# A fused attention-and-MLP decode step with its gradients: one product moved in the forward loop, two stores moved in the backward loop

## The chip, the core and the metric

The kernel runs on one NeuronCore of a Trainium2 chip. Its five engines work side by side, each through its own queue of instructions in order: PE (matrix products), DVE and ACT (vector and scalar work), POOL and SP (here they issue DMAs). Sixteen DMA engines move data between HBM and SBUF. The metric is the device time of one execution in microseconds; lower is better.

## The reference

One token `x` of width D = 640 passes through a layer with adaptive layer norm: attention over a cache, then an MLP. The attention has 32 heads of width 192, and each head has its own K and V cache of 8192 rows. The reference computes the output and the gradients of nine inputs.

```python
def _A_ref(x, k_cache, v_cache, wq, wo):          # 1 query, 32 heads, 8192 rows, 192 wide
    q = (x @ wq).reshape(B, Sq, Hq, Dh) ...
    scores = einsum('bhqd,bhkd->bhqk', q, k) * Dh ** (-0.5)
    p = softmax(scores)
    o = einsum('bhqk,bhkd->bhqd', p, v)
    return o.reshape(B, Sq, Hq * Dh) @ wo
mod = silu(c) @ w_mod                             # sa, ca, ga, sb, cb, gb
h = layernorm(x) * (1 + ca) + sa
x = x + ga * _A_ref(h, K, V, wq, wo)
h = layernorm(x) * (1 + cb) + sb
x = x + gb * _B_ref(h, w1, w2, w3, w4)            # with one token: h + gelu(layernorm(h) @ w3) @ w4
# returned: x, and the gradients of A_x, K, V, wq, wo, w3, w4, c, w_mod for a given grad_out
```

K and V are 2 x 32 x 3.1 MB and must be read; their gradients have the same size and must be written. V is read a second time for the backward part. The gradients of `wq`, `wo` and `w_mod` are outer products of two vectors and are written once each.

## The kernel before

**Layout.** A head's 8192 rows lie on 128 partitions with 64 rows each. A head is loaded in two halves of 32 rows (1.5 MB each); K goes through five such buffers (`KB`), V through three (`VB`).

**Forward loop** (lines 505 to 591, `i` from 0 to 30). The order of the instructions on PE, DVE, ACT and SP is the order of the source lines (`manual_schedule`). An iteration works on three heads at once: the scores of head `i` (`x`), the weighted sums of head `i - 1` (`y`), and the end of head `i - 2` (`z`). The scores of a half are a product on DVE (`dot_mul`, L303), a halving add on DVE (`dot_half`, L308), a sum by matmuls with the identity on PE (`dot_tree`, L314) and a last sum on DVE (`dot_sum`, L318). Softmax takes the maximum through a PE transpose (`mx`, L520) that DVE reads (`negm`, L526), and exponentials on ACT (L349). The weighted V (`scale_v`) is made a quarter at a time, 9 of 16 rows on DVE (L362) and 7 on ACT (L369). For each quarter PE then runs `m_quarter`: the matrix M = K' diag(p) V, which the backward part uses (L384, L389), and the output o (L401). The fourth quarter of a head runs in the next iteration.

In odd iterations from 3 on, the two heads of a pair `t` are finished: `pair_sum` (L438 to 440, PE) sums their outputs into `po`, `pair_o` (L444 to 448, four small DVE operations) divides by the softmax sums, and `pair_ao` (L455, 15 small matmuls) multiplies by the pair's rows of `wo`. The copy of the product (L558, ACT) and the copies of the next query (L273) or modulation (L245) are put into the list `late` and run after the fourth `scale_v`; the products they copy (`q_mm`, L268, in iterations with `i % 4` of 3 and 0; `mod_mm`, L241, at 2, 6 and 10) run where the list is filled. `q_ps` and `mx` share one PSUM buffer (pool `psB`, tag "b", one buffer). SP issues the loads in source order: the next `wo` block (L211) waits until `pair_ao` has read an old one, and the V load of line 582 stands behind it.

**Backward loop** (lines 1231 to 1279, 64 half heads `s`). Each half head needs dP = dO V' (DVE L931, PE L940, DVE L318), then dS (L1239), dK as an outer product on DVE (L956), and dV as outer products on PE (L951) that ACT copies out (L952). Both are stored by DMAs that POOL issues (`store`, L1189), dV of a half head first, and then dK. Beside them runs a list of side jobs, which `slot()` advances in even steps over the half heads: among them `g_chunk`, which turns a loaded block of `wq` or `w_mod` into the block of its gradient in place (in the buffers `w_st` and `stg` in turn) and stores it (L1050). The last two of these blocks are columns 0 and 1 of `w_mod`. POOL also loads rows of probabilities for later half heads (`er_b`, L795).

Of the kernel before, what the change touches and what calls it, by code (L numbers as in the profile page):

```python
# [20 lines left out]
def kernel(  # L21
# [26 lines left out]
    nc = tc.nc  # L48
# [16 lines left out]
    CW = 2 * PW  # L65
# [48 lines left out]
    def tcol(n, name, dtype=FP32):  # L114
        return tmp.tile([P, n], dtype, name=name)
# [81 lines left out]
    dwm_v = out_9.rearrange("(i p) n -> p i n", p=P)  # L197
# [5 lines left out]
    def load_w(view3, lo, hi):  # L203
        w = wst.tile([P, ND, CW], BF16, name="w_st", tag="w", bufs=1)
        nc.sync.dma_start(out=w[:, :, 0 : hi - lo], in_=view3[:, :, lo:hi])
        return w
# [99 lines left out]
    def dot_half(prod):  # L306
        w = DH // 2
        V_.tensor_tensor(out=prod[:, :, 0:w], in0=prod[:, :, 0:w], in1=prod[:, :, w : 2 * w], op=ALU.add)  # L308

    def dot_tree(prod, psR, w):  # L310

        ps = psR.tile([P, JH, TS], FP32, name="dot_ps", tag="d")
        for k in range(0, w, TS):
            T_.matmul(ps, lhsT=ident_bf, rhs=prod[:, :, k : k + TS], start=(k == 0), stop=(k == w - TS))  # L314
        return ps

    def dot_sum(ps, dst):
        V_.reduce_sum(out=dst, in_=ps, axis=AX.X)  # L318
# [20 lines left out]
    with tc.tile_pool(name="vs", bufs=3) as vsp, tc.tile_pool(name="ft", bufs=2) as ft, \  # L339
# [7 lines left out]
        def softmax(h, S_h, negm):  # L347
            E4 = ft.tile([P, J, 4], BF16, name="E4")
            A_.activation(out=E4, in_=S_h[:, :, None].to_broadcast([P, J, 4]), func=ACT.Exp, bias=negm[:, 0:1], scale=1.0)  # L349
            A_.copy(out=E_all[:, h, :], in_=E4[:, :, 0])  # L350
            Ef = ft.tile([P, J], FP32, name="Ef")
            A_.copy(out=Ef, in_=E4[:, :, 0])
            return E4, Ef

        def g_scale_v(q, v, E4, Ef, out, n):
            vs = vsp.tile([P, JQ, VW], BF16, name="vs")
            out.append(vs)
            j0 = q * JQ
            v0 = (q % 2) * JQ
            A_.copy(out=vs[:, :, DH:VW], in_=E4[:, j0 : j0 + JQ, :])  # L360
            if n:
                V_.tensor_tensor(  # L362
                    out=vs[:, 0:n, 0:DH].rearrange("p j (a b) -> p j a b", b=4),
                    in0=v[:, v0 : v0 + n, :].rearrange("p j (a b) -> p j a b", b=4),
                    in1=E4[:, j0 : j0 + n, None, :].to_broadcast([P, n, DH // 4, 4]),
                    op=ALU.mult,
                )
            for k in range(n, JQ):
                A_.activation(out=vs[:, k, 0:DH], in_=v[:, v0 + k, :], func=ACT.Copy, scale=Ef[:, j0 + k : j0 + k + 1])  # L369
                yield  # L370

        def scale_v(q, v, E4, Ef, n=JQ - NVA):
            out = []
            for _ in g_scale_v(q, v, E4, Ef, out, n):
                pass
            return out[0]

        def m_units(q, kb, vs, mp, last=3):
            j0 = (q % 2) * JQ
            z = q == last  # L380

            def main(lo, hi):
                for k in range(lo, hi):
                    T_.matmul(mp[:, 0:MW], lhsT=kb[:, j0 + k, 0:P], rhs=vs[:, k, 0:MW], start=(q == 0 and k == 0), stop=(z and k == JQ - 1), skip_group_check=True)  # L384

            def rest():
                for k in range(JQ):
                    p0 = 64 * (k % 2)
                    T_.matmul(mp[p0 : p0 + 64, MO : MO + MW], lhsT=kb[:, j0 + k, P:DH], rhs=vs[:, k, 0:MW], start=False, stop=(z and k >= JQ - 2), skip_group_check=True)  # L389

            return [lambda: main(0, JQ // 2), lambda: main(JQ // 2, JQ), rest]

        def m_quarter(q, kb, vs, mp, op):
            for f in m_units(q, kb, vs, mp):
                f()
            o_quarter(q, vs, op)

        def o_quarter(q, vs, op):
            for k in range(JQ):
                p0 = 32 * (k % 4)  # L400
                T_.matmul(op[p0 : p0 + 32, 0:MW], lhsT=ones_bf, rhs=vs[:, k, 0:MW], start=(q == 0 and k < 4), stop=(q == 3 and k >= JQ - 4), skip_group_check=True)  # L401
# [40 lines left out]
        def pair_o(t, po):  # L442
            rz = tcol(3, "rz")
            V_.reciprocal(out=rz, in_=po[:, 3:6])  # L444
            V_.tensor_scalar(out=o_col[:, 3 * t : 3 * t + 3], in0=po[:, 0:3], scalar1=rz[:, 0:1], scalar2=None, op0=ALU.mult)
            V_.tensor_copy(out=rinv[:, 2 * t : 2 * t + 2], in_=rz[:, 1:3])
            o2 = ft.tile([P, 3, 2], BF16, name="o2")
            V_.tensor_tensor(out=o2, in0=omask, in1=o_col[:, 3 * t : 3 * t + 3, None].to_broadcast([P, 3, 2]), op=ALU.mult)
            return o2
# [8 lines left out]
        w = load_w(wq_v, 0, CW)  # L458
# [44 lines left out]
        with tc.manual_schedule(engines=ORDER):  # L503
            for i in range(H1):
                x = X.get(i)
                nx = X[i + 1] = {"k": [], "v": []}
                y = X.get(i - 1) if i > 0 else None
# [16 lines left out]
                if y is not None:  # L524
                    negm = tcol(1, "negm")
                    V_.reduce_max(out=negm, in_=mx, axis=AX.X, negate=True)  # L526
                    E4, Ef = softmax(i - 1, y["S"], negm)
# [21 lines left out]
                    m_add(i - 2, z["mp"], mt)  # L549
                dot_half(pb)  # L550
                x["d1"] = dot_tree(pb, psR, DH // 2)
                if last:
                    o2 = pair_o(t, po)
                if y is not None:
                    vs = scale_v(2, y["v"][1], E4, Ef)
                if last:
                    ps_ao = pair_ao(o2, wo_l.pop(t))
                    late.append(lambda ps=ps_ao, t=t: A_.copy(out=AO[:, :, 2 * t : 2 * t + 2], in_=ps))  # L558
# [13 lines left out]
                if i % 4 == 0 and mb < NMB:  # L572
                    nb = min(CW // P, NMB - mb)
                    wch = load_w(wm_v, mb * P, (mb + nb) * P)
                if y is not None:
                    m_quarter(2, y["k"][1], vs, y["mp"], y["op"])
                dot_sum(x["d0"], x["S"][:, 0:JH])
                if y is not None:
                    y["vs"] = scale_v(3, y["v"][1], E4, Ef)
# [16 lines left out]
            x, y, z = X[H1], X[H1 - 1], X[H1 - 2]  # L596
# [191 lines left out]
    NS = 2 * HQ  # L788
# [22 lines left out]
    def transposed(x0, cols, outer, wT):  # L811

        n = min(8, 15 - x0)
        tp = psT.tile([P, 1024], BF16, name="wT_ps", tag="t")
        for x in range(x0, x0 + n):
            b, a = divmod(x, outer)
            for lo, hi, src in cols(a, b):
                T_.transpose(out=tp[lo:hi, (x - x0) * P : (x - x0 + 1) * P], in_=src, identity=ident_bf)  # L818
        A_.copy(out=wT[:, x0 * P : (x0 + n) * P], in_=tp[:, 0 : n * P])  # L819
# [146 lines left out]
    HEADS = ((0, 0, P, 0), (1, 0, 64, P), (2, 0, P, DH), (1, 64, P, DH + P))  # L966
    NWM = NMOD // CW
    GX = -(-2 * ND // 6)
    cur = {}
    wseq = []  # L970

    def next_w():
# [40 lines left out]
    def g_chunk(b, first, v3, rows, dst, n, acc, lay):  # L1013

        lo = n * CW
        if first:
            cur["w"] = cur.pop("next")
        w = stg = cur["w"][:, :, b * PW : (b + 1) * PW]
        cols = lambda a, b_: [(l, r, w[:, a, c0 : c0 + r - l]) for bb, l, r, c0 in lay if bb == b_]
        v_bf = tcol(3, "v_bf", BF16)  # L1020
        V_.tensor_copy(out=v_bf, in_=v3)
        yield
        wT = bst.tile([P, 15 * P], BF16, name="wT", tag="wT")
        transposed(0, cols, ND, wT)
        tp = psS.tile([NF, P], FP32, name="bc_t", tag="s")
        T_.transpose(out=tp[0:3, :], in_=v3, identity=ident_f)
        vrow = tmp.tile([3, P], BF16, name="vrow")
        A_.copy(out=vrow, in_=tp[0:3, :])
        yield
        transposed(8, cols, ND, wT)  # L1030
        bp = psB.tile([P, 512], FP32, name="bc_ps", tag="b")
        for bb, l, r, c0 in lay:
            T_.matmul(bp[:, c0 : c0 + r - l], lhsT=pick(3, bb), rhs=vrow[:, l:r], start=True, stop=True)
        v_bc = bst.tile([P, PW], BF16, name="v_bc")
        A_.copy(out=v_bc, in_=bp[:, 0:PW])
        yield
        ps = psS.tile([P, ND], FP32, name="acc_ps", tag="s")
        for i in range(ND):
            for bb in range(3):
                T_.matmul(ps[:, i : i + 1], lhsT=wT[:, (bb * ND + i) * P : (bb * ND + i + 1) * P], rhs=v_bf[:, bb : bb + 1], start=(bb == 0), stop=(bb == 2))  # L1040
        for i in range(3):
            V_.tensor_scalar(out=stg[:, i, :], in0=v_bc, scalar1=rows[:, i : i + 1], scalar2=None, op0=ALU.mult)
        yield
        V_.tensor_tensor(out=acc, in0=ps, in1=acc, op=ALU.add)
        for i in range(3, ND):
            V_.tensor_scalar(out=stg[:, i, :], in0=v_bc, scalar1=rows[:, i : i + 1], scalar2=None, op0=ALU.mult)
        if first:
            next_w()
        else:
            nc.gpsimd.dma_start(out=dst[:, :, lo : lo + CW], in_=cur["w"])  # L1050
        yield

    def g_dq(t):
# [96 lines left out]
    NP = sum(n for n, _ in jobs)  # L1150
    side = iter(p for _, g in jobs for p in g)
    SLOTS = 4 * (NS - 5)
    prog = [0, 0]
# [77 lines left out]
    for s in range(NS):  # L1231
# [8 lines left out]
            out=dS4,  # L1240
# [36 lines left out]
            dq_cols(s, row)  # L1277
        done_s[0] = s + 1
        slot()
    while prog[1] < NP:  # L1280
        next(side)
        prog[1] += 1


# [28 lines left out]
```

## Time and profile before

| | |
|---|---|
| median of 7 runs | 1438.03 us (1435.35 to 1441.87) |
| profiled execution, its time | 1439.51 us |
| profiled execution, its span | 1437.7 us |
| busy: PE, DVE, ACT, POOL | 1194.2, 1110.4, 878.8, 138.0 us |
| moved by DMA | 571.96 MB, mean 398 GB/s |
| mean granted PE clock | 0.714 |

The span reaches from the first to the last instruction of the trace. Busy times are sums of instruction times, and for PE the ends are modelled. "Idle before" is the time in which an engine stood still ahead of an instruction, with what released it. The chain of work that ended last has PE 36%, DVE 29%, DMA 13%, issue 9% and ACT 9% of the span.

### The profile page before, as it was taken

The numbers are of one execution on the slowest core, as the hardware profiler recorded it, in microseconds if no ns is written. First come the engines' busy times: TensorE is split into PE (matmuls) and PEld (weight loads), VectorE is DVE, ScalarE is ACT, GpSimd is POOL, SyncE is SP. The second block draws the span as 40 slices with busy tenths as digits, with TensorE's granted clock in tenths as the row PEclk, the third lists the DMA queues.
The fourth block names the chain that finished last, engine by engine and source line by source line (L and its number), as shares of the span: only waits on it lengthen the run. The fifth ranks groups of instructions, "written<-read, shape, count | busy, mean of one in ns | idle before, by whom it ended". The sixth has DMA issues, their size and how long they took to land.

```text
span 1437.7 us, 29992 instructions
## 1 busy us (share of the span) xinstructions
PE 1194.2 (83%) x12577; PEld 779.9 (54%) x12577; DVE 1110.4 (77%) x1395; ACT 878.8 (61%) x1923; POOL 138.0 (10%) x240
## 2 busy tenths in 40 slices
PE   3999999999999897888888787877787788778984
PEld 1677777777777676544444444444444444444542
DVE  4999999999999996676766776676677567667683
ACT  0777777677777763545565656556566556555654
POOL 0000000000000000111110111111111111111111
PEclk7999999999999997655555556556556555555555
DMA  9999999999999995699999999999999999999997
GB/s 374 402 419 419 417 417 413 412 407 416 417 410 410 418 382 198 242 399 422 415 403 422 420 413 415 418 419 421 391 417 423 400 414 397 412 383 409 393 412 324
DMA packets 77748, 571.96 MB, mean 398 GB/s; under 512 B 8590, under 2 KB 26718, under 8 KB 37294
## 3 DMA queue, kind: packets, MB, share of 16 engines
q1 hardware_dynamic: 51402, 343.59, 59.0%
q0 software_dynamic: 26192, 226.47, 38.2%
q8 instruction: 98, 1.61, 0.4%
q14 instruction: 36, 0.29, 0.0%
q10 hardware_dynamic: 20, 0.00, 0.0%
HBM read 343.58 MB, written 225.91 MB: 396 GB/s over the span
## 4 chain that ended last, share of the span: by engine, by line
PE 36%; DVE 29%; DMA 13%; issue 9%; ACT 9%; POOL 1%; SPq 0%; ACTq 0%; POOLq 0%; DVEq 0%
PE dot_ps L940 16%; DVE prod L303 9%; DMA out_dram<-KB 7%; PE dv_ps L951 6%; DVE pq L931 5%; DMA KB<-in_A_k_cache_dram 4%; DVE vs L362 4%; PE wT_ps L818 4%; DVE prod L308 4%; ACT vs L369 3%; PE mp L384 3%; PE dot_ps L314 2%; DVE S_h L318 2%; ACT wT L819 2%; PE mp L389 2%
## 5 line engine op out<-in xcount | busy, mean ns | idle before, releaser
L952 ACT CAST KB<-dv_ps 128x768 bf16<-128x768 f32 x504 | 382.6, 804 | 275.4 <-PE dv_ps L951 274.7
L940 PE MATMUL dot_ps<-pq,ident_bf 128*128 128x256 bf16 x1536 | 359.1, 403 | 67.2 <-DVE pq L931 67.0
L369 ACT ACTIVATE vs<-VB,Ef 128x192 bf16<-128x192 bf16 x840 | 303.3, 444 | 0.0
L940 PEld LDWEIGHTS <-ident_bf 128*128 128x128 bf16 x1536 | 188.2, 133 | 193.0 <-issue 131.8
L951 PE MATMUL dv_ps<-do_r,er_b 1*128 1x192 bf16 x2048 | 221.2, 335 | 55.3 <-ACT KB L952 53.2
L956 DVE TENSOR_TENSOR KB<-qs_bc,dS 128x3072 bf16<-128x3072 bf16 x126 | 220.8, 1753 | 28.0 <-DMA out_dram<-KB 22.6
L931 DVE TENSOR_TENSOR pq<-VB,do_r 128x3072 bf16<-128x3072 bf16 x126 | 220.7, 1751 | 0.0
L303 DVE TENSOR_TENSOR prod<-KB,qs_bc 128x6144 bf16<-128x6144 bf16 x62 | 207.9, 3353 | 13.9 <-DMA KB<-in_A_k_cache_dram 7.0
L951 PEld LDWEIGHTS <-er_b 1*128 1x128 bf16 x2048 | 92.4, 111 | 174.7 <-issue 170.2
L384 PE MATMUL mp<-vs,KB 128*128 128x193 bf16 x1920 | 185.5, 249 | 1.2 <-DVE vs L362 0.9
L384 PEld LDWEIGHTS <-KB 128*128 128x128 bf16 x1920 | 165.2, 98 | 18.5 <-issue 7.1
L318 DVE TENSOR_REDUCE dP<-dot_ps 128x32 f32<-128x512 f32 x64 | 44.2, 691 | 143.9 <-PE dot_ps L940 143.9
L795 POOL DMA_DIRECT2D er_b<-er_t x64 | 40.9, 639 | 1160.6 <-PE w3T_ps L667 569.8
L314 PE MATMUL dot_ps<-prod,ident_bf 128*128 128x512 bf16 x372 | 96.2, 397 | 46.1 <-DVE prod L308 46.1
L362 DVE TENSOR_TENSOR vs<-VB,E 128x1728 bf16<-128x1728 bf16 x120 | 123.7, 1052 | 0.0
L308 DVE TENSOR_TENSOR prod<-prod 128x3072 bf16<-128x3072 bf16 x62 | 108.8, 1754 | 1.0
L819 ACT COPY wT<-wT_ps 128x1024 bf16<-128x1024 bf16 x84 | 80.8, 962 | 45.1 <-PE wT_ps L818 43.8
L389 PE MATMUL mp<-vs,KB 128*64 128x193 bf16 x1920 | 103.3, 251 | 0.0
L349 ACT ACTIVATE E<-S_h,negm 128x256 bf16<-128x256 f32 x30 | 15.2, 508 | 143.7 <-DVE negm L526 143.7
L389 PEld LDWEIGHTS <-KB 128*64 128x64 bf16 x1920 | 77.2, 110 | 19.5 <-issue 19.5
L314 PEld LDWEIGHTS <-ident_bf 128*128 128x128 bf16 x372 | 37.4, 106 | 84.3 <-issue 56.8
L1189 POOL DMA_DIRECT2D out_dram<-KB x127 | 68.4, 542 | 43.9 <-ACT KB L952 18.3
(333 smaller groups left out, 1015.2 us busy)
## 6 DMA issues: line engine op xcount, KB each, us to landing
VB<-in_A_v_cache_dram SPq DMA_DIRECT2D x125, 1536.0 KB, 11.8
out_dram<-KB POOLq DMA_DIRECT2D x125, 1536.0 KB, 14.8
KB<-in_A_k_cache_dram SPq DMA_DIRECT2D x64, 1536.0 KB, 11.9
wo_st<-in_A_wo_dram SPq DMA_DIRECT2D x30, 480.0 KB, 11.5
w_st<-in_A_wq_dram SPq DMA_DIRECT2D x12, 960.0 KB, 10.8
out_dram<-wo_st POOLq DMA_DIRECT2D x16, 480.0 KB, 19.4
out_dram<-w_st POOLq DMA_DIRECT2D x7, 960.0 KB, 19.8
w_st<-in_w_mod_dram SPq DMA_DIRECT2D x6, 960.0 KB, 18.7
```

The costliest lines, as they stand in the source:

```text
L303: V_.tensor_tensor(out=prod, in0=src, in1=vec[:, None, :].to_broadcast([P, JH, DH]), op=ALU.mult)
L308: V_.tensor_tensor(out=prod[:, :, 0:w], in0=prod[:, :, 0:w], in1=prod[:, :, w : 2 * w], op=ALU.add)
L314: T_.matmul(ps, lhsT=ident_bf, rhs=prod[:, :, k : k + TS], start=(k == 0), stop=(k == w - TS))
L362: V_.tensor_tensor(out=vs[:, 0:n, 0:DH].rearrange("p j (a b) -> p j a b", b=4), in0=v[:, v0 : v0 + n, :].rearrange("p j (a b) -> p j a b", ...
L369: A_.activation(out=vs[:, k, 0:DH], in_=v[:, v0 + k, :], func=ACT.Copy, scale=Ef[:, j0 + k : j0 + k + 1])
L384: T_.matmul(mp[:, 0:MW], lhsT=kb[:, j0 + k, 0:P], rhs=vs[:, k, 0:MW], start=(q == 0 and k == 0), stop=(z and k == JQ - 1), skip_group_chec ...
L389: T_.matmul(mp[p0 : p0 + 64, MO : MO + MW], lhsT=kb[:, j0 + k, P:DH], rhs=vs[:, k, 0:MW], start=False, stop=(z and k >= JQ - 2), skip_grou ...
L931: V_.tensor_tensor(out=pq[:, q], in0=v_l[s][:, q * JQ : (q + 1) * JQ, :], in1=do_of(ht(s)[0])[:, None, :].to_broadcast([P, JQ, DH]), op=AL ...
L940: T_.matmul(ps[:, q * JQ : (q + 1) * JQ, :], lhsT=ident_bf, rhs=pq[:, q, :, k : k + TS], start=(k == 0), stop=(k == DH - TS), skip_group_c ...
L951: T_.matmul(ps[:, b, k * DH : (k + 1) * DH], lhsT=er[p0 : p0 + 1, 2 * m + k, :], rhs=doh[p0 : p0 + 1, :], start=True, stop=True)
L952: A_.copy(out=dV4[:, 2 * q : 2 * q + 2, m * PW : (m + 1) * PW], in_=ps[:, :, 0:PW])
L956: V_.tensor_tensor(out=dK[:, lo:hi, :].rearrange("p j (a b) -> p j a b", b=4), in0=qh.rearrange("p (a b) -> p a b", b=4)[:, None, :, :].to ...
```

## The change

In the forward loop, `scale_v` of the third quarter goes ahead of `pair_o`, and `m_quarter` of the third quarter goes ahead of `pair_ao`, and with it ahead of the query and modulation products. In the backward loop, the stores of the last two blocks of the gradient of `w_mod` are kept in a list and issued after the dK stores of half heads 60 and 61. The loop that ran left-over side jobs at the end becomes an assertion that none is left.

```diff
@@ forward loop
                 dot_half(pb)
                 x["d1"] = dot_tree(pb, psR, DH // 2)
+                if y is not None:
+                    vs = scale_v(2, y["v"][1], E4, Ef)
                 if last:
                     o2 = pair_o(t, po)
                 if y is not None:
-                    vs = scale_v(2, y["v"][1], E4, Ef)
+                    m_quarter(2, y["k"][1], vs, y["mp"], y["op"])
                 if last:
                     ps_ao = pair_ao(o2, wo_l.pop(t))
                     late.append(lambda ps=ps_ao, t=t: A_.copy(out=AO[:, :, 2 * t : 2 * t + 2], in_=ps))
...
                     wch = load_w(wm_v, mb * P, (mb + nb) * P)
-                if y is not None:
-                    m_quarter(2, y["k"][1], vs, y["mp"], y["op"])
                 dot_sum(x["d0"], x["S"][:, 0:JH])
@@ backward side jobs
-    cur = {}
+    cur, kept = {}, []
@@ g_chunk
-            nc.gpsimd.dma_start(out=dst[:, :, lo : lo + CW], in_=cur["w"])
+            keep = lambda w=cur["w"]: nc.gpsimd.dma_start(out=dst[:, :, lo : lo + CW], in_=w)
+            if dst is dwm_v and n in (GX - 2, GX - 1):
+                kept.append(keep)
+            else:
+                keep()
@@ backward loop
         done_s[0] = s + 1
         slot()
-    while prog[1] < NP:
-        next(side)
-        prog[1] += 1
+        if s in (NS - 4, NS - 3):
+            kept.pop(0)()
+    assert prog[1] == NP and not kept
```

On PE, DVE and POOL the same instructions run in another order; SP's and ACT's queues keep their order.

## The prediction

> **What bounds the kernel now.** I read the page first (parts 1, 2 and 4), then, for each of the two places that the change touches, the engine waits, the instructions in order of time, and stretches with busy times. The page's slices divide the run: about 20 to 545 us is the forward loop over heads with DVE and DMA both at nine tenths or more, 545 to 630 is the middle, and the rest is the backward loop. A forward stretch of two heads, from the busy times by stretch (PE, PE weight loads, DVE, ACT, POOL, clock, DMA share, GB/s):
>
> ```profile
> 350.00:383.00 33.00, 31.16 (x461) 24.19 (x459) 32.22 (x31) 24.48 (x79) 0.00 (x0) 1.00 1.01 419
> ```
>
> DVE is busy 32.2 of 33.0 us, and PE and DMA are close behind. So the DVE queue sets the forward pace and its waits are the time to be had. All of DVE's long waits from 20 to 545 us:
>
> ```profile
> DVE prod L303 <- PE dot_ps L314: 6.7, 5, 2.8
> DVE rz L444 <- ACT vs L369: 4.7, 9, 0.6
> ...
> DVE prod L303 <- DMA KB<-in_A_k_cache_dram: 2.1, 5, 0.5
> DVE rz L444 <- PE op L440: 2.0, 3, 0.9
> DVE negm L526 <- PE mx L520: 1.2, 1, 1.2
> ```
>
> The two rz rows are 6.7 us in 12 odd iterations, and they are one wait, whatever their releaser is called: rz reads what `pair_sum` (L438-440) put into `po`, and it starts 0.49 us after the start of L440 in each case (313.55 and 314.04, 379.54 and 380.03). One case, in DVE's order of time:
>
> ```profile
> 311.80 1.76 DVE L308 TENSOR_TENSOR prod<-prod 128x3072 bf16<-128x3072 bf16 x1
> 314.04 0.18 DVE L444 RECIPROCAL rz<-op 128x3 f32<-128x3 f32 x1 [0.48 <-ACT vs L369]
> ...
> 314.51 0.17 DVE L448 TENSOR_TENSOR o<-omask,o_col 128x6 bf16<-128x6 f32 x1
> 314.59 1.05 DVE L362 TENSOR_TENSOR vs<-VB,E 128x1728 bf16<-128x1728 bf16 x1
> 315.56 0.68 DVE L318 TENSOR_REDUCE S_h<-dot_ps 128x32 f32<-128x512 f32 x1
> ```
>
> The `vs` row behind rz needs nothing from it. PE around the query product of an even iteration:
>
> ```profile
> 299.18 0.98 PE L268 MATMUL q_ps<-w_st,ha_bf 128*128 128x384 bf16 x5
> 300.00 1.51 PE L384 MATMUL mp<-vs,KB 128*128 128x193 bf16 x16
> ...
> 306.16 1.46 PE L314 MATMUL dot_ps<-prod,ident_bf 128*128 128x512 bf16 x6 [0.19 <-DVE prod L308]
> ```
>
> PE has only 0.19 us to spare before the next score tree. In the backward loop no engine waits for a DMA after 1236 us; PE and the hand-overs PE to ACT to PE run the half heads, 10.1 us each at the end (POOL's dV/dK pairs at 1397.62, 1407.75, 1417.83). The end, by stretch:
>
> ```profile
> 1402.00:1406.00 4.00, 4.00 (x25) 2.03 (x24) 1.85 (x2) 2.30 (x3) 0.00 (x0) 0.50 1.03 431
> 1406.00:1409.00 3.00, 1.61 (x18) 0.80 (x18) 2.80 (x4) 2.34 (x4) 1.70 (x3) 0.50 0.47 195
> 1409.00:1416.00 7.00, 7.00 (x40) 3.58 (x39) 4.92 (x3) 3.70 (x5) 0.00 (x0) 0.50 1.01 421
> 1416.00:1419.00 3.00, 1.66 (x17) 0.80 (x17) 2.63 (x3) 2.26 (x4) 1.05 (x2) 0.50 0.11 45
> 1419.00:1433.00 14.00, 2.51 (x20) 1.02 (x19) 1.84 (x2) 4.32 (x6) 1.05 (x2) 0.50 1.00 415
> ```
>
> The DMA engines stand idle 0.53 x 3 = 1.6 us and 0.89 x 3 = 2.7 us, 4.3 us in all, and then drain the last two pairs (6.3 MB) without a gap up to 1434.
>
> **What the Trainium skill says.** TensorE: Matmul & The Clock Gate, "Architectural detail": ACT and DVE are strict FIFO. The trace agrees: `vs` stands behind rz. The same page, Part 1: the clock falls to half when PE idles through a window of some 3.4 us. Here it shows 0.50 for about 3 us near 122, 190 and 504 us in the forward loop, each in a slow pair of heads. DMA: Bandwidth & Descriptors, "Bandwidth": 435 GB/s is the ceiling; the best stretch of 33 us here has 419.
>
> **The change, part by part.** Work is neither added nor removed; three things move.
>
> (1) DVE, odd iterations 3 to 29: the four small operations of `pair_o` go behind the third `vs`. From the end of one halving (306.1) to rz PE takes 314.04 - 306.12 = 7.9 us, DVE needs 313.56 - 306.12 = 7.4. With `vs` (0.97 us from start to start) in between, DVE comes at 8.4, so the wait of about 0.5 is gone with 0.5 to spare. Bounds: 0 and 6.7 us. Seven waits after 300 us (0.48, 0.56, 0.55, 0.56, 0.48, 0.55, 0.86) and the first two (0.56, 0.49) sum to 5.1. The other three (1.6) lie between 111 and 250 us, where DVE also waits for K loads (four of the five, 1.8 us); there I count nothing, since a faster DVE would meet the same loads. K loads land 11.5 us (median) after issue and are used some 12 us after it, and the pace wanted, 33.0/32.5 x 412 GB/s (mean of the bytes from 251 to 449 us) = 418, has been reached, but barely. For new K waits I take off 0.3.
>
> (2) PE: the third M quarter (2.67 us, L384, L389, L401) goes ahead of the 15 `pair_ao` matmuls (0.38) and also of the query product (0.82) or the modulation product of `late`. It need not wait: its `vs` ends before the second score tree does (PE 315.1). After it `pair_ao` finds o2 ready. What it uncovers is `mx` (L520): it shares the one buffer of tag "b" with `q_ps`, so it must wait until ACT has copied q_ps out. The third quarter used to hide that; now it is 0.15 (end of the product) + 0.06 + 0.47 (L273) + 0.05 = 0.7 us of PE in 14 iterations, 9.8 us in all. Behind mx stand the fourth quarter, which frees a K buffer, and the first score tree of the next head. Cover: in i % 4 == 3 the PE idle before that tree (0.88 after i = 15). In i % 4 == 0 only 0.19: the tree comes up to 0.5 us late. Next late would be `prod` (L303, shares its buffer), but DVE has 1.94 us of `vs` before it against 1.46 of tree, which leaves about 0.4. negm needs mx 1.2 us later than it comes now. So I take 0 for these, with 14 x 0.5 = 7 us as the other bound. The exception is i = 28: there the broadcast of dbo already makes negm wait 1.2 us, and q_ps stands before it: +0.45.
>
> On SP, the wo load waits for `pair_ao`, and the V load behind it goes out 1.4 us later (L211, L298); the same holds at i = 2, 4, 6, 8, 10 behind the weight load. That V is used 22 us after its issue and lands in some 11; the next K load on SP comes 4.7 us later. The DMA engines have more than one load in hand then: 0.
>
> (3) Backward: two stores of 0.98 MB leave POOL's queue at 1340.4 and 1368.1 and come back behind the pairs at 1398.7 and 1408.8 (0.9 us of POOL each, POOL then idle for 8 us). Nothing waited for a DMA at the first places, so the gain there is 0. At the new places each takes 0.98 MB / 415 GB/s = 2.4 us, 4.7 together, and the idle DMA time is 4.3: the last two pairs start about 0.5 us later, and the end with them. Bounds: 0 and 4.7 (if nothing fits a gap). The load of er_b at 1406.9 gets behind the first store, but is used only at 1418.3. The buffers of the held stores have no later user.
>
> Sum: -5.1 + 0.3 + 0.45 + 0.5 = -3.85 us. The profiled execution took 1439.5 (span 1437.7 and 1.8 around it), which becomes 1435.7. It is 1.5 above the median of the seven runs, 1438.0, which becomes 1434.2. A gain at the loop's end is kept: the loads of the middle and of the backward loop are issued by the same queues, that much earlier.
>
> **Rivals.**
> - Loads bind the forward loop. For it: DMA share 1.01 and five K waits already. Against it: whole pairs of heads at exactly 33.0 us without a K wait, while DMA moved 407 to 419. Then the rz time turns into K waits, and the tail costs 0.5 to 1: 1437 to 1439.
> - PE binds, the slower side: the uncovered q_ps copy delays the score tree in the iterations with i % 4 == 0 and then DVE. It decides where the PE idle before L314 is under 0.7 us and the 0.4 of DVE's cover is used up, as after a dip of the clock. Price 7 us, with the rz gain lost and the tail: 1443 to 1446. Against it: my count leaves the cover intact.
> - The held stores do relieve the backward loop, by up to their 4.7 us. Against it: no DMA wait after 1236. With the forward gain: 1429 to 1431.
>
> **How the numbers follow.** Forecast (gain of 2.5 to 6): 0.60, own range 1432 to 1435.5. Loads bind: 0.21. PE binds: 0.11. Backward relieved: 0.08. 0.3% (4.3 us, about what a measurement of this kernel can tell from no change) puts the lines at 1433.7 and 1442.3. Faster: half of the forecast and the last rival, 0.38. Slower: 0.11. Same: 0.51. The range 1430.5 to 1439.5 leaves out about half of the last rival, the slower case and little else.
>
> **What would show it.** Right: rz after `vs` with no wait; forward pairs of heads at 32.5 us; mx with waits of 0.5 to 0.7 for L273 on PE, but no new wait of prod L303; the DMA gaps at 1406 and 1416 filled, and the DMA end after the last store 0.5 us later than now. Wrong: DVE waits for K loads growing by several us (loads bind), waits of prod for dot_ps L314 or of negm for mx growing (PE binds), or the backward loop itself shorter between the middle and the last pair. More dips of the clock in the forward loop would spoil the forecast too: each pair of heads with one took over a microsecond more (34.7, 34.8 and 36.4 against 33.0).

## The result and the profile after

The changed kernel takes 1450.98 us (median of 12 runs, 1447.04 to 1459.27) beside 1437.58 us for the kernel before (31 runs). The ratio is 1.0094, with a 95% interval of [1.0075, 1.0114]: it is slower by 13.4 us. The prediction, 1434.2 us with a range up to 1439.5, was wrong in sign. The profiled execution of the changed kernel took 1459.27 us (span 1457.5), the longest of its runs, so its trace shows somewhat more loss than the median has.

First the view that carried the prediction: DVE's waits in the forward loop, 20 to 570 us, of the kernel after. Each row has what waits and for what, the total in us, the number of times and the longest one.

```profile
DVE prod L303 <- ACT qs_bc L273: 15.0, 7, 2.3
DVE prod L303 <- PE dot_ps L314: 8.0, 7, 2.8
DVE negm L526 <- PE mx L520: 3.1, 4, 2.1
DVE S_h L318 <- PE dot_ps L314: 3.0, 3, 2.2
...
DVE prod L303 <- DMA KB<-in_A_k_cache_dram: 1.2, 3, 0.5
...
DVE rz L444 <- PE op L440: 0.2, 1, 0.2
```

The two rz rows that the prediction shows of before (4.7 and 2.0 us) have shrunk to one of 0.2, as they should. In their place is a row that the kernel before does not have: the score product `prod` waits seven times, 2.1 us each, for ACT's copy of the query, L273. One of the seven, the end of iteration 15 and the start of 16, on DVE in order of time:

```profile
282.35 1.05 DVE L362 TENSOR_TENSOR vs<-VB,E 128x1728 bf16<-128x1728 bf16 x1
283.32 0.17 DVE L444 RECIPROCAL rz<-op 128x3 f32<-128x3 f32 x1
...
286.15 0.22 DVE L516 TENSOR_REDUCE m<-S_h 128x1 f32<-128x64 f32 x1
288.38 3.36 DVE L303 TENSOR_TENSOR prod<-KB,qs_bc 128x6144 bf16<-128x6144 bf16 x1 [2.01 <-ACT qs_bc L273]
...
296.41 3.36 DVE L303 TENSOR_TENSOR prod<-KB,qs_bc 128x6144 bf16<-128x6144 bf16 x1 [0.87 <-PE dot_ps L314]
```

rz comes behind `vs` and waits for nothing. Then the first product of the next head stands still for 2.01 us. PE and ACT of the same kernel say why:

```profile
282.49 1.46 PE L314 MATMUL dot_ps<-prod,ident_bf 128*128 128x512 bf16 x6 [0.21 <-DVE prod L308]
283.78 1.51 PE L384 MATMUL mp<-vs,KB 128*128 128x193 bf16 x16
...
286.46 0.53 PE L455 MATMUL ao_ps<-o,wo_st 128*128 128x2 bf16 x15
286.85 0.97 PE L268 MATMUL q_ps<-w_st,ha_bf 128*128 128x384 bf16 x5
288.40 0.49 PE L520 MATMUL mx<-ident_f,m 128*128 128x128 f32 x2 [0.58 <-ACT qs_bc L273]
...
293.66 2.72 PE L314 MATMUL dot_ps<-prod,ident_bf 128*128 128x512 bf16 x6 [2.19 <-DVE prod L308]
```

```profile
287.86 0.49 ACT L273 ACTIVATE qs_bc<-q_ps 128x384 bf16<-128x384 f32 x1 [0.67 <-PE q_ps L268]
```

The same place in the kernel before, PE, ACT and DVE:

```profile
281.15 1.46 PE L314 MATMUL dot_ps<-prod,ident_bf 128*128 128x512 bf16 x6 [0.21 <-DVE prod L308]
282.82 0.97 PE L268 MATMUL q_ps<-w_st,ha_bf 128*128 128x384 bf16 x5
...
283.83 0.49 ACT L273 ACTIVATE qs_bc<-q_ps 128x384 bf16<-128x384 f32 x1 [0.21 <-PE q_ps L268]
...
284.99 3.35 DVE L303 TENSOR_TENSOR prod<-KB,qs_bc 128x6144 bf16<-128x6144 bf16 x1
```

In the changed kernel the query product starts 286.85 - 282.49 = 4.36 us after the start of the score tree; in the kernel before it was 282.82 - 281.15 = 1.67 us. It is 2.69 us later, which is the length of the third M quarter. Before, the copy ended at 283.83 + 0.49 = 284.32 and `prod` began at 284.99, so there were 0.67 us to spare, and 2.69 - 0.67 = 2.02 us is the wait that is seen. The `mx` row has the wait that was predicted, 0.58 us. The last PE row of the changed kernel shows a cost on top: PE, left idle for 2.19 us, runs the next score tree in 2.72 us in place of 1.46, and the second `prod` waits 0.87 us for it. This happened after four of the seven waits; the last section has more on it.

The start of the last `prod` of the loop marks how far the forward part is. It comes 10.3 us later, before and then after:

```profile
527.53 3.35 DVE L303 TENSOR_TENSOR prod<-KB,qs_bc 128x6144 bf16<-128x6144 bf16 x1
```

```profile
537.87 3.35 DVE L303 TENSOR_TENSOR prod<-KB,qs_bc 128x6144 bf16<-128x6144 bf16 x1
```

At the other end, dS of the last half head comes 18.5 us later, and 22.0 us pass from there to the end of the span against 20.7. So of the 19.8 us between the two profiled executions 10.3 lie in the forward loop, 8.2 between it and the last half head, and 1.3 at the tail. The 8.2 us are all lost before half head 56: its dS comes 18.5 us later too (1338.52 and 1357.04). In the kernel before, the first of the two moved stores leaves at 1340.38, so up to there the backward loop runs the same instructions in the same order in both kernels.

The tail of the kernel after, by stretch (the columns are those of the prediction's stretches; the last two are the busy share of the DMA engines and GB/s):

```profile
1424.00:1427.50 3.50, 2.11 (x20) 0.92 (x18) 2.77 (x4) 2.47 (x5) 1.86 (x4) 0.50 0.99 412
1427.50:1434.50 7.00, 7.00 (x40) 3.62 (x39) 4.95 (x3) 3.73 (x5) 0.76 (x1) 0.50 1.03 424
1434.50:1437.50 3.00, 1.69 (x18) 0.80 (x17) 2.60 (x3) 2.23 (x4) 1.08 (x2) 0.50 0.95 372
```

The two idle stretches of the DMA engines (0.47 and 0.11 before) are filled, as predicted.

### The profile page after: what moved, and what is told of

Read it like the earlier page. It is cut to its first block, busy times and chain, and to the rows that moved or that the text cites. A ratio compares the mean times of both kernels' runs of the same rounds, so it can differ in the third digit from the quotient of the medians.

```text
span 1457.5 us, 29991 instructions
## 1 busy us (share of the span) xinstructions
PE 1197.1 (82%) x12577; PEld 777.6 (53%) x12577; DVE 1110.4 (76%) x1395; ACT 881.5 (60%) x1923; POOL 137.9 (9%) x240
## 4 chain that ended last, share of the span: by engine, by line
PE 39%; DVE 27%; DMA 18%; ACT 7%; issue 7%; POOL 1%; SPq 0%; POOLq 0%; ACTq 0%; DVEq 0%
PE dot_ps L940 15%; DVE prod L303 8%; DMA out_dram<-KB 8%; PE dv_ps L951 5%; DVE pq L931 5%; PE mp L384 4%; DVE prod L308 4%; PE dot_ps L314 4%; PE wT_ps L818 3%; DVE vs L362 3%; PE mp L389 2%; DMA KB<-in_A_k_cache_dram 2%; DMA er_b<-er_t 2%; ACT vs L369 2%; DMA wo_st<-in_A_wo_dram 2%
## 5 line engine op out<-in xcount | busy, mean ns | idle before, releaser
L940 PE MATMUL dot_ps<-pq,ident_bf 128*128 128x256 bf16 x1536 | 362.9, 407 | 67.1 <-DVE pq L931 66.9
L956 DVE TENSOR_TENSOR KB<-qs_bc,dS 128x3072 bf16<-128x3072 bf16 x126 | 220.8, 1753 | 34.8 <-DMA out_dram<-KB 31.9
L303 DVE TENSOR_TENSOR prod<-KB,qs_bc 128x6144 bf16<-128x6144 bf16 x62 | 207.9, 3354 | 29.4 <-ACT qs_bc L273 15.0
## 6 DMA issues: line engine op xcount, KB each, us to landing
VB<-in_A_v_cache_dram SPq DMA_DIRECT2D x125, 1536.0 KB, 11.3
w_st<-in_A_wq_dram SPq DMA_DIRECT2D x12, 960.0 KB, 11.3
out_dram<-wo_st POOLq DMA_DIRECT2D x16, 480.0 KB, 20.7
```

The source lines that it names most:

```text
L303: V_.tensor_tensor(out=prod, in0=src, in1=vec[:, None, :].to_broadcast([P, JH, DH]), op=ALU.mult)
L940: T_.matmul(ps[:, q * JQ : (q + 1) * JQ, :], lhsT=ident_bf, rhs=pq[:, q, :, k : k + TS], start=(k == 0), stop=(k == DH - TS), skip_group_c ...
L956: V_.tensor_tensor(out=dK[:, lo:hi, :].rearrange("p j (a b) -> p j a b", b=4), in0=qh.rearrange("p (a b) -> p a b", b=4)[:, None, :, :].to ...
```

## The experiments

The theory formed from the trace: the query comes late for the next head's product on DVE, and that is the forward loss. The rivals: the held stores cost the time; PE binds through the uncovered copy ahead of `mx`; the place of `pair_ao` and of the loads behind it matters. And one question was open: where the 4.35 us gain of the forward loop went. Each ratio below is to the kernel before and has its 95% interval in brackets; it is not exactly the quotient of the two medians.

**Each part alone.** fwd_only has the three moves in the forward loop and the backward loop of before; bwd_only has the held stores alone.

```diff
 # fwd_only: of the change, this hunk only
+                if y is not None:
+                    vs = scale_v(2, y["v"][1], E4, Ef)
                 if last:
                     o2 = pair_o(t, po)
                 if y is not None:
-                    vs = scale_v(2, y["v"][1], E4, Ef)
+                    m_quarter(2, y["k"][1], vs, y["mp"], y["op"])
...
-                if y is not None:
-                    m_quarter(2, y["k"][1], vs, y["mp"], y["op"])
```

> The forward part of the change alone; POOL's stores as in the kernel before. Theory A (the query product behind the third M quarter is late for the next head's product on DVE): nearly the whole loss is here, +9 to +11 us against before at the end of the forward loop, with seven waits of prod L303 for ACT qs_bc L273 of about 2.1 us each. Theory B (the held stores cost the time in the backward loop): within 3 us of the kernel before.

```diff
 # bwd_only: of the change, the hunks of the backward loop only
+            if dst is dwm_v and n in (GX - 2, GX - 1):
+                kept.append(keep)
...
+        if s in (NS - 4, NS - 3):
+            kept.pop(0)()
```

> The backward part alone; the forward loop as before. Theory A: -1 to +1.5 us: the stores fill the 4.3 us of idle DMA time near the end and nothing else moves. Theory B: +3 to +8 us, which is what the changed kernel's profile shows beyond the 9.6 us of its forward loop.

Measured: fwd_only 1447.56 us (4 runs), ratio 1.0079 [1.0056, 1.0102], which is +11.3 us; the last forward `prod` 11.6 us later than before, with 14.7 us of waits for L273 in 7 places. bwd_only 1439.51 us, ratio 1.002 [1.0004, 1.0037], +2.9 us with an interval of 0.6 to 5.3, which lies between its two theories and excludes neither. The forward part carries some four fifths of the loss, and the two add up to 14.2 beside 13.4 for the whole change.

**The wait for the query taken away, all else kept.** stale_q is the whole change, but heads 4, 8 and so on up to 28 take the query of the head four before, which has long been there. The edit is to the changed kernel.

```diff
-                qh = qs_bc[:, i * DH : (i + 1) * DH]
+                iq = i - 4 if i % 4 == 0 and i else i
+                qh = qs_bc[:, iq * DH : (iq + 1) * DH]
```

> The changed kernel, but heads 4, 8, ... 28 take the query of the head four before them, which has long been copied (so their scores and all that follows from them are those of another query; the work is the same). Only the wait of prod L303 for the copy L273 goes; the wait of mx for the same copy stays. Theory A: the seven waits are gone, the forward loop ends 3 to 7 us earlier than in the kernel before, the total is -6 to 0 us against it. If instead mx, the later wo loads or the place of the third quarter cost the time (theory C), it stays +8 us or more.

Measured: 1436.25 us, ratio 1.0005 [0.9986, 1.0024]. Without this one wait the changed kernel can't be told from the one before. The last forward `prod` comes 1.5 us earlier than before, not the 3 to 7 that were expected. The waits of DVE in the forward loop of stale_q:

```profile
DVE prod L303 <- DMA KB<-in_A_k_cache_dram: 8.4, 16, 1.2
DVE prod L303 <- PE dot_ps L314: 6.8, 5, 2.8
...
DVE rz L444 <- PE op L440: 0.2, 1, 0.2
```

The row for L273 is gone and that for rz is 0.2, but the waits for K loads are 8.4 us, where before has 2.1.

The same with the backward loop of before is stale_fwd (its line numbers from 512 on are one higher):

> The forward part of the change alone, with the query of heads 4, 8 and so on up to 28 replaced by that of the head four before (another computation: seven of the 32 heads get a wrong query); the backward loop is as before. Theory: with the wait for the query gone and no held stores the time is below before, by the 2 us of the forward loop that stale_q showed: 1434 to 1437 beside 1437.5, and 1 to 3 us below the stale_q run's distance to before. Rival (the held stores cost nothing, and the remainder of stale_q is from the forward loop): as stale_q, within 1 us of before.

Measured: 1435.25 us beside 1435.8, ratio 0.9996 [0.9979, 1.0014]; the last forward `prod` 4.1 us earlier than before, K waits 7.7 us. The expected gains over before and over stale_q are of the size of these intervals, so neither is confirmed. What the run settles is `mx`. PE's waits in its forward loop:

```profile
PE dot_ps L314 <- DVE prod L308: 38.0, 26, 5.2
PE mx L521 <- ACT qs_bc L273: 7.4, 13, 0.6
```

The 7.4 us that PE waits ahead of `mx` are the same as in the changed kernel, and yet no loss is seen, and DVE's waits for PE did not grow: 5.3 us for the score tree (6.7 before) and 1.2 for `mx` (1.2 before). This wait is covered. The rival by which PE binds through it, at 7 us, is refuted.

**The query's place alone, both ways.** q_behind is the kernel before with only the query and modulation products put behind the third M quarter; `pair_o` and `pair_ao` stay.

```diff
                     ps_ao = pair_ao(o2, wo_l.pop(t))
                     late.append(lambda ps=ps_ao, t=t: A_.copy(out=AO[:, :, 2 * t : 2 * t + 2], in_=ps))
+                if y is not None:
+                    m_quarter(2, y["k"][1], vs, y["mp"], y["op"])
                 if i % 4 == 3 and wch is not None:
...
-                if y is not None:
-                    m_quarter(2, y["k"][1], vs, y["mp"], y["op"])
```

> The kernel before with one thing moved: the query and modulation products go behind the third M quarter; pair_o, the third vs and pair_ao stay where they were. Theory A: seven waits of prod L303 for L273 of 1.5 to 2.3 us, and +11 to +17 us in all, more than the full change because the waits of rz stay. Theory C (pair_ao behind the quarter, and with it the wo and V loads on SP): 0 to +3 us.

q_first is the opposite: the forward part of the change with the query and modulation products left ahead of the third M quarter.

```diff
+                if y is not None:
+                    vs = scale_v(2, y["v"][1], E4, Ef)
                 if last:
                     o2 = pair_o(t, po)
-                if y is not None:
-                    vs = scale_v(2, y["v"][1], E4, Ef)
-                if last:
-                    ps_ao = pair_ao(o2, wo_l.pop(t))
...
                 if i % 4 == 2 and wch is not None:
                     late.append(lambda ps=mod_mm(nb, wch), lo=mb, n=nb: mod_out(lo, n, ps))
...
+                if y is not None:
+                    m_quarter(2, y["k"][1], vs, y["mp"], y["op"])
+                if last:
+                    ps_ao = pair_ao(o2, wo_l.pop(t))
...
-                if y is not None:
-                    m_quarter(2, y["k"][1], vs, y["mp"], y["op"])
```

> The forward part of the change with one difference: the query and modulation products stay ahead of the third M quarter, and only pair_ao goes behind it; the backward loop is as before. Theory (the query's place is the whole forward loss): no wait of prod for qs_bc, no dips that follow it, the end of the forward loop 1 to 4 us earlier than before, 1433.5 to 1437 beside 1437.5. Rival (pair_ao and with it the wo and V loads, 1.4 us later on SP, are part of the loss): slower than before by 1 to 4 us, with waits of DVE or PE for V or for dot_ps.

Measured: q_behind 1454.44 us (4 runs), ratio 1.0119 [1.0087, 1.0152], by the medians 18.0 us and so a little over the expected 11 to 17; q_first 1436.2 us beside 1435.8, ratio 1.0004 [0.999, 1.0018]. The trace of q_behind is of the fastest of its runs, 1446.23 us; its last forward `prod` comes 14.3 us later than before. DVE's forward waits of q_behind:

```profile
DVE prod L303 <- ACT qs_bc L273: 13.7, 7, 2.0
...
DVE rz L444 <- ACT vs L369: 5.1, 8, 0.9
DVE rz L444 <- PE op L440: 4.4, 6, 0.9
```

q_behind has the loss without any other part of the change, and it keeps the rz waits. q_first has every other forward move, and no loss is seen; its interval leaves room for at most 2.6 us. So the place of `pair_ao`, with the wo and V loads behind it, is not what cost the 11 us. Nor does q_first have the gain that was expected of it: its last forward `prod` comes only 1.1 us earlier, and K waits are 5.6 us.

**Where the rz gain goes.** vs_first is the kernel before with only `scale_v(2)` put ahead of `pair_o`, the one edit that removes the rz waits.

```diff
+                if y is not None:
+                    vs = scale_v(2, y["v"][1], E4, Ef)
                 if last:
                     o2 = pair_o(t, po)
-                if y is not None:
-                    vs = scale_v(2, y["v"][1], E4, Ef)
```

> The kernel before with the third scale_v ahead of pair_o as the only edit; no product moves, the backward loop is as before. Theory (the late query is the loss, and the rz waits are a true but small gain): no wait of prod for qs_bc, the rz waits of 6.7 us gone, but only a part of them kept, because the stale_q run got 8.4 us of K waits in their place; K waits of DVE 4 to 8 us against 2.1, the end of the forward loop 1 to 4 us earlier, 1433.5 to 1437 beside 1437.5 for before. Rival (loads bind the forward loop): K waits up by the whole 6 us, the end of the forward loop within 1 us of before, time within 1 us of before. Rival (vs ahead of pair_o is itself harmful, because o2 and pair_ao come 1 us later): PE waits for o2, the score tree is late, 1438 to 1441.

Measured: 1435.07 us beside 1435.8, ratio 0.9987 [0.9968, 1.0006]. The forward end is 6.0 us earlier in this trace and 3.8 in that of vs_tail below, whose forward loop is the same; bwd_only and bwd_late, whose forward loop is that of before, show 1.6 and 1.0 us by chance alone. Against these two that is 2 to 5 us; but q_first, stale_q and stale_fwd, which have this edit among others, end only 1.1, 1.5 and 4.1 us earlier. So some part of the 4.35 us may be there, and it is too little for these times to tell from nothing. DVE's forward waits of vs_first:

```profile
DVE prod L303 <- DMA KB<-in_A_k_cache_dram: 5.6, 11, 0.9
DVE prod L303 <- PE dot_ps L314: 5.2, 4, 2.8
...
DVE rz L444 <- PE op L440: 0.2, 1, 0.2
```

To see whether the loads take the rest, the same edit was made on a base with less to load. nowo loads only the first two wo blocks and uses the second again for all later pairs; nowo_vs adds the edit of vs_first.

```diff
-                    wo_l[(i + 1) // 2] = load_wo((i + 1) // 2)
+                    wo_l[(i + 1) // 2] = load_wo((i + 1) // 2) if i < 3 else wo_l[(i - 1) // 2]
```

> The kernel before with less DMA in the forward loop: only the wo blocks of the first two pairs are loaded, and the other pairs' products use the second block again (so the attention's output and what follows from it are of another computation). 14 loads of 0.49 MB, 1.2 us of DMA each or 3.6% of a pair of heads, are gone; every engine's instructions stay. It is the base for nowo_vs. K waits of DVE go from 2.1 us to under 1, the rz waits of 6.7 us stay, the forward loop ends 1 to 4 us earlier: 1432 to 1437 beside 1437.

> nowo with the third scale_v ahead of pair_o (the one edit of vs_first; again only two wo blocks are loaded, so another computation). Theory (in vs_first the DMA engines at 411 to 419 GB/s took most of the freed rz time back as K waits): with 3.6% less to load, K waits stay under 2 us and the forward loop ends 4 to 7 us earlier than nowo's, against a part of that in vs_first; the time is 4 to 7 us below nowo's. Rival (the rz time goes elsewhere, to waits of prod for dot_ps or to PE): the forward loop ends within 2 us of nowo's although there are no K waits.

Measured: nowo 1432.04 us, ratio 0.9976 [0.9956, 0.9996]; nowo_vs 1428.33 us, ratio 0.9946 [0.9928, 0.9965], both against the kernel before. The last forward `prod` comes 5.3 and 10.7 us earlier than before; for nowo that is more than the expected 1 to 4. DVE's forward waits of nowo, and then of nowo_vs:

```profile
DVE rz L444 <- ACT vs L369: 6.6, 12, 0.6
```

```profile
DVE prod L303 <- DMA KB<-in_A_k_cache_dram: 2.2, 7, 0.4
...
DVE rz L444 <- PE op L440: 0.2, 1, 0.2
```

With 3.6% less to load the edit brings the forward end forward by 5.5 us, and the median falls by 3.7 us, with K waits at 2.2 us where vs_first has 5.6. The forward end agrees with the expectation; the median lies just under its 4 to 7, and the K waits just over the 2 us expected. That waits for loads come in the place of rz waits is shown by the K rows: 5.6 to 8.4 us in vs_first, vs_tail, q_first, stale_fwd and stale_q, all without rz waits, and 2.1, 4.0 and 2.7 in before, bwd_only and bwd_late, whose forward loop is that of before. How much of the gain they take is not settled: the gain in time of vs_first over before and that of nowo_vs over nowo agree within their intervals.

**The tail.** bwd_late holds the two stores two half heads longer, behind the very last pairs. The edit is to bwd_only.

```diff
-        if s in (NS - 4, NS - 3):
+        if s in (NS - 2, NS - 1):
             kept.pop(0)()
```

> The kernel before with the two stores held longer still: they are issued after the dK stores of the last two half heads, 62 and 63, in place of 60 and 61. Theory (what is held is paid at the end in so far as it fills no idle time of the DMA engines; here the idle 1.7 and 2.7 us near the end lie mostly before the stores): the time from dS of the last half head to the end grows from 20.7 us by about 4.7 us (1.97 MB at 415 GB/s), to 24.5 to 25.5, against 22.3 in bwd_only; 4 to 6 us slower than before, 1440.5 to 1443 beside 1436.5. Rival (the cost of bwd_only is in DMA waits inside the backward loop, not in the drain at the end): the tail stays within 1.5 us of bwd_only's 22.3 and the time within 1.5 us of its 1.002.

vs_tail goes the other way: vs_first, with dV and dK of the last two half heads stored in two quarters, so that the DMA engines have work earlier.

```diff
-                    store(dV_hd, s, dV, JQ if s == 0 else 0, JH)
-                elif n == 3 and s == 0:
+                    store(dV_hd, s, dV, JQ if s == 0 or s >= NS - 2 else 0, JH)
+                elif n == 3 and (s == 0 or s >= NS - 2):
...
-        if s < 2:
+        if s < 2 or s >= NS - 2:
             store(dK_hd, s, dK, 0, JQ)
...
-        store(dK_hd, s, dK, JQ if s < 2 else 0, JH)
+        store(dK_hd, s, dK, JQ if s < 2 or s >= NS - 2 else 0, JH)
```

> vs_first, and the dK and dV of the last two half heads are stored in two quarters each, so that the first halves leave earlier and fill the DMA engines' last idle stretch (2.7 us in before). Theory (the end is the drain of the last two pairs, and DMA idle time just ahead of it is worth its own length): vs_first's time less 1 to 2.5 us, the time from dS of the last half head to the end 18.5 to 20 us against 20.7. Rival (the first half of the last pair can't leave before the DMA is busy with the pair before, so no idle time is filled): as vs_first, within 0.7 us. Rival (more and smaller stores cost POOL and the DMA engines time): 1 us or more above vs_first.

Measured: bwd_late 1447.85 us (6 runs) beside 1436.02, ratio 1.0097 [1.0062, 1.0133]; vs_tail 1433.51 us beside 1435.8, ratio 0.9998 [0.9979, 1.0016]. The time from dS of the last half head to the end of the span is 20.7 us before, 22.3 in bwd_only, 26.6 in bwd_late, 20.8 in vs_first and 19.1 in vs_tail. The stores at the end of bwd_late, POOL in order of time:

```profile
1424.91 1.06 POOL L1193 DMA_DIRECT2D out_dram<-KB  x2 [9.00 <-ACT KB L952]
1425.96 0.89 POOL L1050 DMA_DIRECT2D out_dram<-stg  x1
1430.69 1.08 POOL L1193 DMA_DIRECT2D out_dram<-KB  x2 [3.84 <-ACT KB L952]
1431.76 0.87 POOL L1050 DMA_DIRECT2D out_dram<-w_st  x1
```

Put behind the last idle time of the DMA engines, the two stores lengthen the tail by 5.9 us, somewhat more than the 4.7 of their bytes; put where they fill it, by 1.6; and filling it with the last pairs themselves shortens the tail by 1.7 us. So the end is the drain of what is left, and the mechanism of the prediction's third part holds. Two things do not fit. bwd_late as a whole lost 11.8 us, not 4 to 6: its six runs fall into two groups, three at 1442 to 1444 us and three at 1452 to 1453, and the profiled one is of the upper group, with dS of the last half head 7.1 us later than before and 37.1 us of waits of dK (L956) for the stores out of its buffers, against 22.6 before. Up to the first held store the instructions are those of before in the same order, so this is not explained by anything that was moved; it stays open. And the 1.7 us of vs_tail can't be told from nothing in its time: its median is 1.6 us below that of vs_first, but its ratio to before is the higher of the two, 0.9998 beside 0.9987. No version that loads all it needs is shown to beat the kernel before; vs_first and vs_tail are level with it.

## Why the prediction was wrong

**(1) DVE: the wait went as predicted, the gain is not shown.** rz behind `vs` has no wait. Of the 4.35 us that the forward loop was to gain, the five versions with this edit and no wait for the query show 1.1 to 6.0 us at the loop's end in single traces, where two with the forward loop of before show 1.0 and 1.6, and vs_first has 0.13% [-0.06, 0.32] in its time. The term that was mis-sized is the +0.3 for new K waits: in those five versions they grew by 3.5 to 6.3 us over the 2.1 of before (in the changed kernel itself, where DVE stands for the query, they are 1.2). This is the first rival, loads bind the forward loop, for this part of the change. The Trainium skill (DMA: Bandwidth & Descriptors, "Bandwidth") has a ceiling of 435 GB/s; in vs_first, vs_tail and stale_q the loop held 410 to 419 GB/s over stretches of 66 to 131 us, and the step assumed that it could run at 418 throughout.

**(2) PE: the step that failed.** It asked what the later place of the query product uncovers, and its answer was "What it uncovers is `mx` (L520)". It had found the next user of the buffer that the product is written to and missed the reader of the data; the PE lines that it shows for this step are of an even iteration. In iterations with `i % 4` of 3 the copy L273 writes the query of heads `i + 1` and `i + 2`, and the first product of the next iteration on DVE, `prod` (L303), reads it. The spare time was 0.67 us, by two rows of the trace of before, and the move takes 2.69. That makes 2.02 us in each of 7 iterations, 14.1 us; the trace has 15.0. The sum of the step with this term: DVE's forward waits changed by +15.0 for the query, +1.3 for dot_ps, +1.9 for `mx`, +0.4 for S_h, -6.7 for rz and -0.9 for K, together +11.0 us; the last `prod` came 10.3 us later. The +1.3 for dot_ps goes with the dips of the clock, five in the loop in place of three (the last section), which the prediction had named as able to spoil it. In the iterations with `i % 4` of 0 the copied query is that of heads `i + 2` and `i + 3`, needed two iterations on, and no wait came of it.

What the step did say came true: 13 waits of `mx` of 0.6 us, and no cost of them is seen (stale_fwd). The rival that ended on the slower side had the place right, PE's later query product, but the wrong mechanism: it let the loss come in iterations with `i % 4` of 0 by way of the score tree. The signs to watch for named "no new wait of prod L303" outright, and it is there that the trace contradicted the prediction. That no load suffers from the later place of `pair_ao` was not contradicted (q_first, to within 2.6 us).

**(3) Backward: right mechanism, and nearly the right size at the tail.** Predicted +0.5; the drain after the last pair went from 10.3 us (1423.61 to 1433.9) to 11.0 (1442.13 to 1453.1), +0.7, and a further 0.6 us came after the last byte (3.8 to 4.4), which no step had. The whole part cost 2.9 us [0.6, 5.3]. In its trace 1.6 us of that are the tail, and another 0.6 lie between half heads 56 and 63; but in the changed kernel that stretch took the same time as before, 78.46 and 78.45 us. The 8.2 us which the profiled execution of the changed kernel lost between the forward loop and the last half head came before half head 56, and so before any moved store. With them go longer waits of dK (L956, DVE) for the stores out of its buffers, 31.9 us against 22.6. But these waits go from 14.2 us (vs_tail) to 42.0 (nowo, which is faster than before) over the runs, and identical stretches of the backward loop differ by several us from one trace to the next: dS of half head 48 stands 4.1 us earlier in bwd_only and 2.7 later in bwd_late than before, with the same instructions in the same order up to there. Why they differ stays open.

## What to carry to other kernels

When an instruction is moved back, follow what it produces to every reader, on every engine, and write down for each the spare time in the trace; a buffer that is shared shows only one of the readers. A reader in the next iteration of the loop is the easiest to miss, because the source text has it far above. And a wait that is removed from an engine pays only as far as the next resource has room. Here, with DMA at 410 to 419 GB/s, 6.7 us of rz waits went and waits for K loads of 5.6 to 8.4 us stood where 2.1 to 4.0 had been.

## What the hardware showed beside that

After a short idle time of PE its granted clock can fall. The kernel after, by stretch around the late score tree:

```profile
290.00:292.00 2.00, 1.47 (x35) 1.03 (x34) 2.00 (x3) 0.03 (x1) 0.00 (x0) 1.00 1.02 421
292.00:294.00 2.00, 0.34 (x1) 0.10 (x1) 2.00 (x2) 1.97 (x7) 0.00 (x0) 0.86 1.03 418
294.00:296.00 2.00, 2.00 (x6) 0.73 (x5) 1.54 (x2) 2.00 (x8) 0.00 (x0) 0.50 1.01 424
296.00:298.00 2.00, 2.00 (x19) 1.62 (x19) 1.59 (x1) 2.00 (x7) 0.00 (x0) 0.78 1.03 434
```

PE stood idle for 2.19 us before 293.66, and the granted clock was 0.50 from 294 to 296 us while PE was fully busy. The Trainium skill (TensorE: Matmul & The Clock Gate, Part 1) lets the clock halve after an idle window of some 3.4 us; here the unbroken idle stretch was shorter than that, after one of 0.58 us some 5 us earlier, and the measurement decides. It is no rule either: the trace has seven idle stretches of 2.19 us, one after each wait for the query. The clock was at 0.50 right after four of them (at 89, 294, 430 and 499 us) and stayed at 1.00 after three (157, 226 and 362 us). It fell to 0.50 at 516 us too, where PE had only stood three times in a row for 0.35 to 0.67 us. What decides is open. After the four dips DVE's second `prod` waited 0.87, 0.87, 0.25 and 0.67 us for the score tree. So a wait of 2 us on another engine that leaves PE idle can cost up to 0.9 us more than itself.
